# Products of the second transform step over both parts at once, and a filter spectrum split by channels between two homes

## The chip, the cores and the metric

The kernel runs on one core of a Trainium2 chip. In the profile the core shows as PE (TensorE: matmuls; PEld are its weight loads), DVE (VectorE), ACT (ScalarE), POOL (GpSimd) and SP, which here only issues DMA transfers. PSUM is used as eight banks of 512 fp32 values per partition. The metric is the device time of one execution in microseconds (us); a kernel's time is the median over its executions. All data are fp32.

## The reference

Two blocks follow each other. The first is a long convolution by FFT, with a filter that a small network makes from position embeddings; the second applies a wide layer with the activation h·cos(h) to each token.

```python
# x, v: (4, 12480, 128); pos_emb: (12480, 64); w1: (64, 64); w2: (64, 128)
h_filt = (np.maximum(pos_emb @ w1, 0.0) @ w2) * np.exp(-0.01 * pos)[:, None]
u = x * v
y = irfft(rfft(u, n=2*S, axis=1) * rfft(h_filt, n=2*S, axis=0)[None], n=2*S, axis=1)[:, :S]
a = (x * y).reshape(49920, 128)
h = a @ w_in                      # w_in: (128, 2048)
out = (h * np.cos(h)) @ w_out     # w_out: (2048, 128)
```

## The kernel before, in words

**The transform.** Sequence positions are taken as `R` = 104 rows of `N2` = 120. A transform has two matmul steps, of sizes `N1` = 96 and `N2` = 120, and two more lead back. The 128 channels are held as `CB` = 64 pairs (`b`), the two channels of a pair (`i`) beside each other. The filter keeps its first 10400 taps, in `FR` = 96 rows. Before the first step, sums and differences of mirrored positions are formed (`u_sums`, `filter_out`), so that the first step leaves `KE` = 124 rows: 0 to 63 from the sums, 64 to 123 from the differences.

**First step** (`f1_mm`, L400; evictions L415 and L424). For each pair two matmuls fill one bank with 96 frequencies `k`, real and imaginary part `r`, for both channels. ACT or DVE, chosen by `f1_takers`, copies it out: one copy for rows 0 to 63, and for rows 64 to 123 a copy and a negated copy, since the parts change places there. For data this goes to `parts`, columns 0 to 191 of the large tile `slots` (128 partitions x 64 pairs x 240 columns x 2). For the filter (`f1_evict_filter`) each pair's 192 columns are divided by frequency: 144 go to a separate tile `ftile`, and the last 48, the imaginary parts with `k` >= `KF` = 48, to `above`, the last 48 columns of `slots`. The filter's eviction therefore takes five instructions, two copies for the upper rows and three for the lower.

**Second step** (`f2_mm`, L437). For two frequencies `k1`, `k1+1` at a time (a unit `j`, 48 of them per batch), a weight tile `w` of 124 x 120 per frequency multiplies the 256 values of that frequency (2 parts x 64 pairs x 2 channels). The result of frequency `g` of the two stands in half `g` of a bank, ordered part, pair, channel. For the filter, one matmul does it where both parts lie in `ftile` (`k` < 48), and two of 128 columns where the imaginary part lies in `above`.

**The product** (`f2_product`, L451). With u the data's result in PSUM and h the filter's in SBUF, the complex product is written back over `parts`: four DVE multiplications of 256 values (two into the place of the result, y, two into a scratch tile `t`), and on POOL one subtraction and one addition of 256 values (L461). `t` has one buffer, and POOL's operation is issued right behind the second and the fourth multiplication.

**What runs in which order.** Every engine works through its own instructions in the order in which the program lists them. `units` (L514) interleaves the parts of a loop: in unit `j` it issues the preparation of unit `j + ahead`, the matmuls of `j`, and between them, at each `yield`, a piece of the eviction of `j - 1`. The program's stages are:

1. Loads of x and v for batch 0 and their product (`first_u`, on POOL and DVE), beside the filter's small network.
2. First step of the filter (L843 to L854): while `first_u` lasts, two pieces of it per piece of `first_u`; then the rest, with the tables of the way back (`inverse_tables`, computed by POOL, and by a Sin on ACT) put in between, and stored to DRAM (L269).
3. First step of batch 0 (L871), beside the conversion of `w_in` from double precision.
4. Second step of batch 0 and of the filter together (`f2_both_units`, L594). Per unit `make_w` makes the next unit's `w` in two buffers (two ACT and two DVE instructions, L289 and L291); `w` is stored to DRAM for the later batches (`wd`, L603), the filter's scaled spectrum is evicted by ACT (L614) and stored too (`hd`, L616), and the product follows. The tables of the way back were reloaded just before (`back_tables`, L874 to L876).
5. Way back of batch 0, first part (L889), beside the conversion of `w_out` and some tables for the second part.
6. The second block. Each of its steps has an up-matmul (L727), ACT L730, DVE L733, POOL L736, ACT L741, DVE L743 and a down-matmul (L752) four steps later. The convolution of the other batches is issued in between, by fixed step costs (`owed`, L942 to L944). There `f2_units` (L575) loads `w` and `h` again and makes the same product, 3 x 48 times.

Of the kernel before, what the change touches and what calls it, by code (L numbers as in the profile page):

```python
# [16 lines left out]
P = 128  # L17
# [13 lines left out]
def kernel(  # L31
# [62 lines left out]
    KF = N1 - 2 * (N2 - N1)  # L94
    CB = D // 2
    assert R * N2 == S and S + TAPS - 1 <= 2 * M and math.exp(DECAY * TAPS) < 2.0 ** -150
    assert D == P and DFF % P == 0 and FO * 2 == P and N1 % 2 == 0 and R <= P
    assert NCH * ROWS <= FR <= R and H <= ODD and KE <= N1 + KF and H <= CB and N2 <= P
# [5 lines left out]
    NALL = 1 + math.ceil((NROWS - R) / P)  # L104
    assert G == 2 * UA and H % UA == 0 and N2 % G == 0
# [4 lines left out]
    hd = dram.tile([N1 // 2, N2, 2, 2, D], F32, name="hd")  # L110
# [141 lines left out]
    def inverse_tables(pool):  # L252

        t = Tables(pool, nc.gpsimd, 4)
        part = t.whole([P, 1], [[1, 1]], channel_multiplier=1, name="part")
        part4 = t.whole([P, 1], [[1, 1]], base=1, channel_multiplier=4, name="part4")
        step = t.whole([P, P], [[1, P]], name="step")
        mid = t.whole([P, P], [[1, P]], base=-MID, name="mid")
        cs, rows, tw_t = back_tables(pool)
        yield from t.sines(step, part, N2, [(cs[:, 0, 0:H + 1], 1), (cs[:, 1, 0:H + 1], 0)],  # L260
                           eighths=slice(0, H + 1, H))
        yield from t.sines(step[:, 1:H], part, N2,
                           [(cs[:, 0, H + 1:], 0), (cs[:, 1, H + 1:], 1)])
        yield from t.sines(step, part4, 4 * N1,
                           [(rows[:, i, :], q) for i, q in enumerate((0, 1, 2, 3))])
        yield from t.sines(mid, part4, TURN, [(tw_t[:, 0, :], 1), (tw_t[:, 1, :], 0)],
                           eighths=slice(H - 1, N2, H))
        t.finish(len(t.waiting))
        for kept, made in ((csd, cs), (rowsd, rows), (twd, tw_t)):  # L269
            nc.sync.dma_start(kept[:, :, :], made[:, :, :])  # L270

    def back_tables(pool):

        cs = pool.tile([N2, 2, N2], F32, name="cs")
# [3 lines left out]
        return cs, rows, tw_t  # L278
# [97 lines left out]
    def clear_gap(u):  # L376

        nc.gpsimd.memset(u[:, :, H:ODD, :], 0.0)
# [45 lines left out]
    def f1_evict_filter(ps, b, share):  # L424

        copy, negated = f1_takers(b, share)
        pj = ps[:, 0:4 * N1].rearrange("p (i k) -> p k i", i=2)
        near, far = ftile[:, b, :, :], above[:, b, :, :]
        copy(out=near[0:ODD], in_=pj[0:ODD, 0:N1 + KF])
        copy(out=far[0:ODD], in_=pj[0:ODD, N1 + KF:])  # L430
        yield
        copy(out=near[ODD:KE, 0:N1], in_=pj[ODD:KE, N1:])
        negated(near[ODD:KE, N1:], pj[ODD:KE, 0:KF])
        negated(far[ODD:KE], pj[ODD:KE, KF:N1])
        yield

    def f2_mm(ps, w, k1, i, filt=False):  # L437

        k = k1 + i
        pi = ps[0:N2, i * 2 * D:(i + 1) * 2 * D]  # L440
        if not filt:
            nc.tensor.matmul(pi, w[:, i, :], parts[0:KE, :, k], start=True, stop=True)  # L442
        elif k < KF:
            both = ftile[0:KE, :, k:k + N1 + 1:N1, :].rearrange("p b r i -> p r b i")
            nc.tensor.matmul(pi, w[:, i, :], both, start=True, stop=True)
        else:
            for r, src in enumerate((ftile[0:KE, :, k, :], above[0:KE, :, k - KF, :])):
                nc.tensor.matmul(pi[:, r * D:(r + 1) * D], w[:, i, :], src,
                                 start=True, stop=True)

    def f2_product(pool, ps, h, k1):  # L451

        y = parts[0:N2, :, k1:k1 + 2, :, :].rearrange("p r k b i -> p r b k i")
        uu, hh = (a.rearrange("p g r (b i) -> p r b g i", i=2) for a in (
            ps[0:N2, :].rearrange("p (g r d) -> p g r d", g=2, r=2), h[:, :, :, :]))
        t = pool.tile([N2, 2, CB, 2, 2], F32, name="t", bufs=1)
        for r, op in ((0, ALU.subtract), (1, ALU.add)):
            nc.vector.tensor_tensor(y[:, r], uu[:, 0], hh[:, r], op=ALU.mult)
            yield
            nc.vector.tensor_tensor(t[:, r], uu[:, 1], hh[:, 1 - r], op=ALU.mult)  # L460
# [105 lines left out]
    def f1_units(bank, u, share=0.5, evict=f1_evict):  # L566
        def mm(j, ps, i):
            if i == 0:
                ps = bank()
            f1_mm(ps, u, j, i)  # L570
            return ps

        return units(CB, F1_STEPS, lambda j: None, mm, lambda j, ps: evict(ps, j, share), 2)

    def f2_units(bank):  # L575
        with tc.tile_pool(name="there", bufs=3) as pool:
            ws, hs = {}, {}

            def before(j):
                ws[j] = pool.tile([KE, 2, N2], F32, name="w")  # L580
                nc.sync.dma_start(ws[j][:, :, :], wd[j, :, :, :])
                hs[j] = pool.tile([N2, 2, 2, D], F32, name="h")
# [11 lines left out]
    def f2_both_units(bank):  # L594

        with tc.tile_pool(name="both", bufs=2) as pool:
# [15 lines left out]
            def after(j, ps):  # L612
                h = pool.tile([N2, 2, 2, D], F32, name="h", bufs=3)
                nc.scalar.activation(h[:, :, :, :].rearrange("p g r d -> p (g r d)"),  # L614
# [169 lines left out]
    with tc.manual_schedule():  # L784
        with tc.tile_pool(name="psum", bufs=8, space=PSUM) as psum, \
# [50 lines left out]
            ftile = fpool.tile([P, CB, N1 + KF, 2], F32, name="ftile")  # L836
            clear_gap(ftile[0:FR, :, :, :])
            with tc.tile_pool(name="out", bufs=1, side="right") as pool:
                for j in range(H // 2):
                    filter_out(pool, bank, aT, ftile, j, w2_sb)  # L840
                    for _ in range(1 + (j % 3 == 0)):
                        next(first_u)
            f1 = f1_units(bank, ftile[0:FR, :, :, :], 0.53, f1_evict_filter)  # L843
# [30 lines left out]
            cs, rows, tw_t = back_tables(lpool)  # L874
            for kept, here in ((csd, cs), (rowsd, rows), (twd, tw_t)):
                nc.sync.dma_start(here[:, :, :], kept[:, :, :])  # L876
# [4 lines left out]
            wpool = ctx.enter_context(tc.tile_pool(name="weights", bufs=1))  # L881
            ident = wpool.tile([P, P], F32, name="ident")
# [92 lines left out]
```

## Time and profile before

| | us |
|---|---|
| median of 7 executions | 3787.01 (3785.79 to 3789.98) |
| the profiled execution | 3786.39 |
| its span, first to last instruction | 3784.6 |
| first step of the filter | about 65 to 122 |
| first step of batch 0 | about 122 to 171 |
| second step of batch 0 and filter | about 172 to 275 |
| way back of batch 0, first part | about 275 to 340 |
| second block, with the other batches until about 2970 | 345 to the end |

The profile describes one execution. A row of a timeline reads: start, duration, engine, line, operation, what it writes and reads, its shape, and how many in a row; in brackets, how long the engine had been idle and what ended that. The chain of waits follows the work that ended last back from the end. A table by stretches of time gives each engine's busy time, the clock granted to PE, the mean busy share of the 16 DMA engines, and the data rate. PE's matmuls overlap and their ends are modelled, so that a short pause of PE can hide in its busy time; the distance from one start to the next is more exact.

### The profile page before, as it was taken

Reading aid. Unit: us, or ns where it says so; the run is one execution under the profiler, and the core shown is the slowest. Engines: PE = TensorE matmul, PEld = TensorE weight load, DVE = VectorE, ACT = ScalarE, POOL = GpSimd, SP = SyncE. Lnnn points to the kernel's source line nnn. Section 1 sums busy time; section 2 is a strip of 40 time slices with the busy share of each in tenths; the row PEclk is TensorE's granted clock in tenths of the full one; section 3 lists DMA queues with packets and bytes.
Section 4 is the critical chain, followed back from the end, with each engine's and each line's share of the span. In section 5 each row is a group of like instructions: output and inputs, shape, how many; then the busy total and the mean of one; then the engine's idle time right before and its main releaser. Section 6 shows DMA issues by size and latency. Waiting matters only on the chain.

```text
span 3784.6 us, 47244 instructions
## 1 busy us (share of the span) xinstructions
PE 3701.5 (98%) x13546; PEld 2109.7 (56%) x13546; DVE 2771.4 (73%) x5658; ACT 2523.7 (67%) x4683; POOL 2589.3 (68%) x2342
## 2 busy tenths in 40 slices
PE   7898999999999999999999999999999999999999
PEld 6777555655466555555565556555566544444444
DVE  7887887688866777788767786788765566666666
ACT  5757776766665557766655567666664677777777
POOL 7667886488854665688745664788644577777776
PEclk9999999999999999999999999999999999999999
DMA  6263542022202550122203540122105200000000
GB/s 166 67 181 105 148 147 58 17 71 79 74 18 67 175 163 28 32 78 77 60 18 109 173 128 16 53 76 78 41 12 167 88 19 21 17 20 20 17 21 14
DMA packets 209499, 276.14 MB, mean 73 GB/s; under 512 B 17111, under 2 KB 146535, under 8 KB 209111
## 3 DMA queue, kind: packets, MB, share of 16 engines
q1 hardware_dynamic: 209239, 273.12, 25.0%
q8 instruction: 109, 1.79, 0.2%
q14 instruction: 151, 1.24, 0.1%
HBM read 193.64 MB, written 79.42 MB: 72 GB/s over the span
## 4 chain that ended last, share of the span: by engine, by line
PE 83%; POOL 7%; DVE 3%; ACT 2%; DMA 2%; issue 2%; SPq 0%; POOLq 0%; DVEq 0%; ACTq 0%
PE ph L727 31%; PE acc L752 27%; PE cv L752 5%; PE cv L491 4%; PE cv L466 4%; POOL f L736 4%; PE cv L402 3%; PE cv L442 3%; PE ph L126 2%; PE ps L442 1%; PE ps L402 1%; POOL tm L295 1%; DMA tm<-td 1%; ACT cs L741 1%; DVE k L733 1%
## 5 line engine op out<-in xcount | busy, mean ns | idle before, releaser
L736 POOL TENSOR_TENSOR f<-a,k 128x512 f32<-128x512 f32 (+1 forms) x1568 | 1985.3, 1266 | 1054.5 <-DVE k L733 1049.9
L727 PE MATMUL ph<-at,w_in_sb 128*128 128x512 f32 (+1 forms) x3136 | 1599.0, 591 | 6.0 <-DVE gt L743 5.4
L730 ACT ACTIVATE a<-ph,quarter 128x512 f32<-128x512 f32 (+1 forms) x1568 | 1072.5, 684 | 759.3 <-PE ph L727 750.5
L752 PE MATMUL acc<-gt,w_out_sb 128*128 128x512 f32 (+1 forms) x2688 | 1375.1, 593 | 9.8 <-ACT ot L758 9.5
L743 DVE TENSOR_TENSOR gt<-ph,cs 128x512 f32<-128x512 f32 (+1 forms) x1568 | 1077.8, 687 | 317.8 <-ACT cs L741 290.3
L733 DVE TENSOR_SCALAR k<-a 128x512 f32<-128x512 f32 (+1 forms) x1568 | 770.1, 491 | 621.2 <-ACT a L730 605.3
L741 ACT ACTIVATE cs<-f 128x512 f32<-128x512 f32 (+1 forms) x1568 | 980.3, 625 | 331.7 <-POOL f L736 329.1
L752 PEld LDWEIGHTS acc<-gt,w_out_sb 128*128 128x128 f32 x2688 | 506.5, 189 | 661.7 <-issue 618.8
L727 PEld LDWEIGHTS ph<-at,w_in_sb 128*128 128x128 f32 x3136 | 554.2, 190 | 337.9 <-issue 268.4
L461 POOL TENSOR_TENSOR slots<-slots,t 120x256 f32<-120x256 f32 x384 | 311.3, 817 | 61.0 <-DVE t L460 38.3
L491 PEld LDWEIGHTS cv<-slots,tm 96*104 96x104 f32 x1920 | 239.5, 170 | 112.0 <-issue 82.1
L491 PE MATMUL cv<-slots,tm 96*104 96x128 f32 x1920 | 253.6, 274 | 12.4 <-DMA tm<-td 6.3
L752 PE MATMUL cv<-gt,w_out_sb 128*128 128x512 f32 (+1 forms) x448 | 224.6, 584 | 0.7 <-DVE gt L743 0.7
L466 PEld LDWEIGHTS cv<-cs,slots 120*96 120x96 f32 x1536 | 176.8, 167 | 67.5 <-issue 65.6
L466 PE MATMUL cv<-cs,slots 120*96 120x120 f32 x1536 | 183.1, 266 | 0.0
L442 PE MATMUL cv<-slots,w 124*120 124x256 f32 x576 | 173.1, 381 | 0.0
L442 PEld LDWEIGHTS cv<-slots,w 124*120 124x120 f32 x576 | 103.7, 184 | 123.7 <-issue 110.7
L402 PEld LDWEIGHTS cv<-c,slots 104*124 104x124 f32 x768 | 132.6, 192 | 71.1 <-issue 58.3
L402 PE MATMUL cv<-c,slots 104*124 104x192 f32 x768 | 151.3, 327 | 4.8 <-DVE gt L743 3.5
L752 PEld LDWEIGHTS cv<-gt,w_out_sb 128*128 128x128 f32 x448 | 84.9, 190 | 104.4 <-issue 99.5
L390 DVE TENSOR_TENSOR xt<-xt,vt 104x256 f32<-104x256 f32 x177 | 137.9, 786 | 0.2 <-DMA vt<-in_v_dram 0.2
L476 DVE TENSOR_TENSOR slots<-cv,other 96x240 f32<-96x240 f32 x384 | 133.5, 394 | 4.2 <-ACT other L474 4.2
(129 smaller groups left out, 2583.6 us busy)
## 6 DMA issues: line engine op xcount, KB each, us to landing
h<-hd SPq DMA_DIRECT2D x144, 240.0 KB
tm<-td SPq DMA_DIRECT2D x96, 312.0 KB
xt<-in_x_dram SPq DMA_DIRECT2D x120, 208.0 KB
vt<-in_v_dram SPq DMA_DIRECT2D x120, 208.0 KB
xs<-in_x_dram SPq DMA_DIRECT2D x120, 208.0 KB
zd<-zs SPq DMA_DIRECT2D x119, 208.0 KB
zb<-zd SPq DMA_DIRECT2D x96, 256.0 KB
w<-wd SPq DMA_DIRECT2D x144, 116.2 KB
```

Of the source, the lines that this page charges most:

```text
L402: nc.tensor.matmul(ps[0:KE, i * 2 * N1:(i + 1) * 2 * N1], u[:, b, 0:KE, i], c1[0:u.shape[0], :, :].rearrange("p r k -> p (r k)"), start=Tr ...
L442: nc.tensor.matmul(pi, w[:, i, :], parts[0:KE, :, k], start=True, stop=True)
L461: nc.gpsimd.tensor_tensor(y[:, r], y[:, r], t[:, r], op=op)
L466: nc.tensor.matmul(ps[0:N1, (i * 2 + r) * N2:(i * 2 + r + 1) * N2], parts[0:N2, r, :, b, i], cs[:, r, :], start=True, stop=True)
L491: nc.tensor.matmul(ps[0:R, i * D:(i + 1) * D], t[:, i, r, :], slots[0:N1, :, place, :], start=(r == 0), stop=(r == 1))
L727: nc.tensor.matmul(ph[:, 0:m], w_in_sb[:, c * P:(c + 1) * P], ats[n][:, 0:m], start=True, stop=True)
L730: nc.scalar.activation(a[:, 0:m], ph[:, 0:m], AF.Identity, bias=quarter[:, 0:1], scale=INV_TWO_PI)
L733: nc.vector.tensor_scalar(out=k[:, 0:m], in0=a[:, 0:m], scalar1=ROUND, scalar2=ROUND, op0=ALU.add, op1=ALU.subtract)
L736: nc.gpsimd.tensor_tensor(f[:, 0:m], a[:, 0:m], k[:, 0:m], op=ALU.subtract)
L741: nc.scalar.activation(cs[:, 0:m], f[:, 0:m], AF.Sin, scale=TWO_PI)
L743: nc.vector.tensor_tensor(gt[:, 0:m], ph[:, 0:m], cs[:, 0:m], op=ALU.mult)
L752: nc.tensor.matmul(accs[n][:, 0:m], w_out_sb[:, c, :], gt[:, 0:m], start=(c == 0), stop=(c == NFC - 1))
```

## The change

- **Product.** Two DVE multiplications of 512 values take the place of four of 256: one forms the result of u's real part with both parts of h, the other that of u's imaginary part with both parts in reversed order. Each reads its part of u from PSUM twice, through a pattern with a step of zero. POOL's two operations stay; both now come behind both multiplications, one `yield` apart. `t` gets two buffers.
- **Order in the bank.** The bank now holds part, pair, frequency, channel, so that what one multiplication reads is contiguous. Each second-step matmul therefore writes runs of two values at a distance of four. `h` in SBUF and `hd` in DRAM take the same order; their sizes stay.
- **Filter's first step.** The two homes are divided by channels: pairs 0 to 47 lie whole in `ftile` (`fout`), pairs 48 to 63 in `above`, each in four pieces. An eviction takes three instructions. The pairs are worked from 63 down, since `fout` lies over the memory of the inputs `fin`. A filter's second-step matmul is always two, of 192 and of 64 columns.
- **Tables.** Of the tables of the way back, only `cs` is reloaded before the joint second step; `rows` and `tw_t` are loaded after it, ahead of `w_in`.

```diff
     def f1_evict_filter(ps, b, share):
         copy, negated = f1_takers(b, share)
-        pj = ps[:, 0:4 * N1].rearrange("p (i k) -> p k i", i=2)
-        near, far = ftile[:, b, :, :], above[:, b, :, :]
-        copy(out=near[0:ODD], in_=pj[0:ODD, 0:N1 + KF])
-        copy(out=far[0:ODD], in_=pj[0:ODD, N1 + KF:])
+        pj = ps[:, 0:4 * N1].rearrange("p (i r q k) -> p r q k i", i=2, r=2, q=SPLIT // 2)
+        if b < NF:
+            there = fout[:, b, :, :].rearrange("p (r q k) i -> p r q k i", r=2, q=SPLIT // 2)
+        else:
+            there = above[:, (b - NF) * SPLIT:(b - NF + 1) * SPLIT, :, :].rearrange(
+                "p (r q) k i -> p r q k i", r=2)
...
+        copy(out=merged(there[0:ODD]), in_=merged(pj[0:ODD]))
         yield
-        copy(out=near[ODD:KE, 0:N1], in_=pj[ODD:KE, N1:])
-        negated(near[ODD:KE, N1:], pj[ODD:KE, 0:KF])
-        negated(far[ODD:KE], pj[ODD:KE, KF:N1])
+        copy(out=there[ODD:KE, 0], in_=pj[ODD:KE, 1])
+        negated(there[ODD:KE, 1], pj[ODD:KE, 0])
         yield
     def f2_mm(ps, w, k1, i, filt=False):
         k = k1 + i
-        pi = ps[0:N2, i * 2 * D:(i + 1) * 2 * D]
+        pi = ps[0:N2, :].rearrange("p (r b g i) -> p g r b i", r=2, g=2, i=2)[:, i]
         if not filt:
             nc.tensor.matmul(pi, w[:, i, :], parts[0:KE, :, k], start=True, stop=True)
-        elif k < KF:
-            both = ftile[0:KE, :, k:k + N1 + 1:N1, :].rearrange("p b r i -> p r b i")
-            nc.tensor.matmul(pi, w[:, i, :], both, start=True, stop=True)
-        else:
-            for r, src in enumerate((ftile[0:KE, :, k, :], above[0:KE, :, k - KF, :])):
-                nc.tensor.matmul(pi[:, r * D:(r + 1) * D], w[:, i, :], src,
-                                 start=True, stop=True)
+            return
+        nc.tensor.matmul(pi[:, :, 0:NF], w[:, i, :],
+                         fout[0:KE, :, k:k + N1 + 1:N1, :].rearrange("p b r i -> p r b i"),
+                         start=True, stop=True)
+        q, m = divmod(k, 2 * (N2 - N1))
+        far = above[0:KE, :, m, :].rearrange("p (b r q) i -> p q r b i", r=2, q=SPLIT // 2)
+        nc.tensor.matmul(pi[:, :, NF:], w[:, i, :], far[:, q], start=True, stop=True)
     def f2_product(pool, ps, h, k1):
-        y = parts[0:N2, :, k1:k1 + 2, :, :].rearrange("p r k b i -> p r b k i")
-        uu, hh = (a.rearrange("p g r (b i) -> p r b g i", i=2) for a in (
-            ps[0:N2, :].rearrange("p (g r d) -> p g r d", g=2, r=2), h[:, :, :, :]))
-        t = pool.tile([N2, 2, CB, 2, 2], F32, name="t", bufs=1)
+        y = parts[0:N2, :, k1:k1 + 2, :, :].rearrange("p r k b i -> p r b (k i)")
+        t = pool.tile([N2, 2, CB, 4], F32, name="t", bufs=2)
+        for r, (dst, hh) in enumerate(((y, h[:, :, :, :]), (t[:, :, :, :], h[:, ::-1, :, :]))):
+            u = ps[0:N2, r * 2 * D:(r + 1) * 2 * D].rearrange("p (b j) -> p b j", j=4)
+            twice = bass.AP(tensor=u.tensor, offset=u.offset, ap=[u.ap[0], [0, 2], *u.ap[1:]])
+            nc.vector.tensor_tensor(dst, twice, hh, op=ALU.mult)
+            yield
         for r, op in ((0, ALU.subtract), (1, ALU.add)):
-            nc.vector.tensor_tensor(y[:, r], uu[:, 0], hh[:, r], op=ALU.mult)
-            yield
-            nc.vector.tensor_tensor(t[:, r], uu[:, 1], hh[:, 1 - r], op=ALU.mult)
             nc.gpsimd.tensor_tensor(y[:, r], y[:, r], t[:, r], op=op)
             yield
...
-            f1 = f1_units(bank, ftile[0:FR, :, :, :], 0.53, f1_evict_filter)
+            f1 = f1_units(bank, fin[0:FR, :, :, :], 0.53, f1_evict_filter,
+                          range(CB - 1, -1, -1))
...
-            cs, rows, tw_t = back_tables(lpool)
-            for kept, here in ((csd, cs), (rowsd, rows), (twd, tw_t)):
-                nc.sync.dma_start(here[:, :, :], kept[:, :, :])
+            cs = third_table(lpool)
+            nc.sync.dma_start(cs[:, :, :], csd[:, :, :])
             for _ in f2_both_units(bank):
                 pass
             first.close()
             wpool = ctx.enter_context(tc.tile_pool(name="weights", bufs=1))
+            rows, tw_t = last_tables(wpool)
+            for kept, here in ((rowsd, rows), (twd, tw_t)):
+                nc.sync.dma_start(here[:, :, :], kept[:, :, :])
```

## The prediction

> **What bounds the kernel now.** First the page's busy times and its chain, then the busy times by stretches: the first two lines below are joint second steps (DVE and DMA busy, PE waiting), the last two second steps inside the second block.
>
> ```profile
> PE 3701.5 (98%) x13546; PEld 2109.7 (56%) x13546; DVE 2771.4 (73%) x5658; ACT 2523.7 (67%) x4683; POOL 2589.3 (68%) x2342
> ...
> PE 83%; POOL 7%; DVE 3%; ACT 2%; DMA 2%; issue 2%; SPq 0%; POOLq 0%; DVEq 0%; ACTq 0%
> ```
>
> ```profile
> 190.00:220.00 30.00, 29.17 (x118) 19.86 (x117) 28.30 (x89) 17.96 (x43) 20.91 (x30) 1.00 0.62 180
> 220.00:243.00 23.00, 22.93 (x136) 18.83 (x135) 22.17 (x69) 14.20 (x36) 16.06 (x23) 1.00 0.61 179
> ...
> 755.00:825.00 70.00, 70.00 (x199) 35.68 (x198) 55.71 (x110) 46.17 (x75) 58.87 (x55) 1.00 0.24 69
> 825.00:895.00 70.00, 70.00 (x198) 35.44 (x197) 56.32 (x115) 46.65 (x74) 62.09 (x58) 1.00 0.27 77
> ```
>
> In the second block PE is busy 70.00 of 70 us while DVE does these products; three of the four batches lie there. So only what lies before about 350 us can shorten much, and I read the timeline of one joint second step, which shows what ends the waits:
>
> ```profile
> 241.91 0.60 ACT L614 ACTIVATE h<-ps 120x512 f32<-120x512 f32 x1 [1.01 <-DMA hd<-h]
> ...
> 243.82 0.59 DVE L291 SCALAR_TENSOR_TENSOR w<-even,tw_w,ps 124x120 f32<-124x120 f32 x2 [0.80 <-DMA wd<-w]
> 244.33 0.42 DVE L458 TENSOR_TENSOR slots<-ps,h 120x256 f32<-120x256 f32 x1
> 244.66 0.41 DVE L460 TENSOR_TENSOR t<-ps,h 120x256 f32<-120x256 f32 x1
> 244.99 0.41 DVE L458 TENSOR_TENSOR slots<-ps,h 120x256 f32<-120x256 f32 x1
> 245.22 1.43 POOL L461 TENSOR_TENSOR slots<-slots,t 120x256 f32<-120x256 f32 x2 [1.30 <-DVE t L460]
> 245.32 0.41 DVE L460 TENSOR_TENSOR t<-ps,h 120x256 f32<-120x256 f32 x1
> 245.84 0.59 DVE L291 SCALAR_TENSOR_TENSOR w<-even,tw_w,ps 124x120 f32<-124x120 f32 x2
> ```
>
> A unit takes 2.02 us (243.82 to 245.84), and three loops have that length. (a) DVE: w, w, four products, and a wait instruction, without a gap. (b) t: POOL 1.43, then t 0.42 (one buffer), then 0.17 of hand-over. (c) The store of `w`: its tile has two buffers, so `w` of unit j+2 waits until the store of unit j has landed. In the trace's landing records four reports end each such store (fifteen that of an h), the last 3.28 us after its issue; from unit 17 on every `w` starts 0.12 us after the last report of the store two units before. Around: 0.12 + 0.61 (both halves of `w` and the issue) + 3.28 = 4.01 for two units. And the packets under way fall below four at no time from 182 to 200 us and stand at exactly four for 7 to 11% of it: some four DMA engines never rest. An engine that serves both stores has 124 / 4 = 31 packets of 960 B at 44 ns and 120 / 15 = 8 of 2 KB at 84 ns in a unit: 2.04 us.
>
> The chain shows the rest: how the first step of the filter ends.
>
> ```profile
> 120.21 0.44 POOL turned L217
> ...
> 120.68 0.30 ACT tw_t L226
> ...
> 122.20 36.02 PE ps L402 x200
> ```
>
> POOL's tables (97.9 to 120.6, without a gap) hold a Sin on ACT, and two evictions behind that Sin hold PE.
>
> **The change, part by part.** Sums are against the profiled execution: 3786.39 us, span 3784.6 and 1.8 around it; the median, 3787.01, is 0.6 above it.
>
> *Products beside the second block.* Removed: per unit four multiplications of 0.415 (row L458/L460); added: two of 512 values. The nearest row, 128x512 with one operand in PSUM (L743), is 0.687. DVE is relieved of 4 × 0.415 − 2 × 0.687 = 0.29 us, 144 times, 41 us. On the path: nothing; PE covers it. If that cover were gone, DVE would still have 14 of 70 us free. POOL's two operations (0.73 to 0.86) now come one behind the other: they can hold the block's L736 for 1.7 instead of 0.86 us. In these stretches a down-matmul starts at least 2.8 us after its DVE result is there, so no PE wait: 0.
>
> *Joint second step, length of a unit.* (a) by start-to-start distances: the products took 0.34 + 0.33 + 0.33 + 0.42 and the wait 0.10; two of 512 take 0.60 + 0.68 + 0.10: 1.88 in place of 2.02. (b) goes, with the second buffer. (c) stays: the same stores of the same sizes, on the same queue. Late next is thus the store, and a unit remains 2.01. Ends: 0, and 0.13 × 44 units = 5.7 gained. I take 0.4, for the first five units alone: there the reports come after 2.8 to 2.9 us and DVE sets the pace (its w starts at 178.09, 180.02, 182.04). [...]
>
> *Its matmuls.* For k < 48 a pass of 256 columns (0.217 from start to start, L445) becomes one of 192 (0.162, L402) and one of 64, bounded by half of the 128-column pass (0.054) and all of it (0.109, L448): 0 to 0.054 more per pass, four per unit, at most 0.22. PE then needs 8 × 0.217 = 1.74 to 1.96 of the 2.01: 0, covered by the store. In the other 24 units two passes of 128 become the same two: no more than that. [...]
>
> *Strided writes to PSUM.* No row of the trace has a matmul that writes with gaps. Lower end 0: a moving operand read in pairs with gaps (L442, 256 columns, 0.217) costs what a contiguous one does (L352, 0.215). Upper end: twice, as if each pair cost two; 576 passes in the second block × 0.217 = 125 us. I take 0, by L442.
>
> *End of the joint step.* After the last `w` (268.33) three rounds of loop (b) follow; POOL ends at 275.34, and the way back waits for it. Without (b): last h at 270.96 to 271.56, products to 272.87, POOL 1.42 and 0.14: 274.43. −0.9; ends: 0 if h still comes late behind a store, −1.5.
>
> *Filter's first step.* DVE per pair, start to start: 0.37 + 0.25 + 0.28 + 0.17 + 0.29 = 1.37 (88.04 to 89.41); afterwards as in the evictions of data, which have the same three shapes: 0.56 + 0.28 + 0.36 = 1.20. ACT: 1.17 to 1.05. Times 31 and 33: 5.3 and 4.0 us. From 74 to 98 us DVE is busy for 23.24 of 24 us, and `u_sums` of batch 0 queues behind these evictions, which delays the loads of x and v and so POOL; 12 DVE evictions lie there: 12 × 0.17 = 2.0. The remaining 19 are hidden by POOL's tables, whose 22.8 us stay and only begin earlier. Behind the last Sin two ACT evictions: 0.2. Sum −2.2; ends 0 (the loads of v, 3.2 us each, hold POOL too, at 67, 72 and 78 us) and −5.5.
>
> *Tables.* Two transfers leave SP's queue ahead of the joint step, where the first `w` waits for ACT; two join it behind the last `hd` and ahead of `w_in`'s, 0.35 us of issue each. First reader: ACT at 278.66; they land about 2.4 us after issue (as at 171 us), before 277. `w_in` and the raw `w_out` come 0.7 later, read first at 283.12: 0; at worst +0.7.
>
> Sum: −2.2 − 0.4 − 0.9 = −3.5: 3782.9 for the profiled execution, 3783.5 for the median.
>
> **Rivals.** *Faster: the store is not the floor.* With landing after 2.85 us loop (c) takes 1.79 a unit, DVE's 1.88 rules: 5.7 more, 3777.8. For: units 2 to 5. Against: the engines that never rest. *No gain in the first step:* v's loads and POOL hold it as before; 3785.7. For: three load waits in the chain; against: DVE's closed row after 80 us. *Slower: PE writes PSUM in pairs more slowly.* At a tenth more, 576 × 0.022 = 12.5: 3796. It decides from 19 ns a pass on (11 us, the 3.5 gained and 7.6 of bound). For: no row excludes it. Against: a pass takes 0.85 ns per column whatever the pattern it reads (L442, L352, L448). *The products shorten the second block:* 41 us of DVE, but PE has no idle time there to give: no price.
>
> **How the numbers follow.** Chances: forecast 0.52, no gain in the first step 0.17, store not the floor 0.19, slow writes 0.12. What a measurement can tell from no change is 0.2%, 7.6 us: below 3779.4 or above 3794.6. Faster: 0.19 and the forecast's edge where the first step gains all 5.5 and the end 1.5, 0.05: 0.24. Slower 0.12. Same 0.64. The forecast's own range is 3779 to 3787; for 8 in 10 it is opened to 3775, past most of the faster case, and to 3790, with 0.12 left out above and 0.06 below.
>
> **What would show it.** After: L458's successor at 120x512, 0.68 us, 384 of them; joint step still 2.0 us a unit, `w` waiting for `wd<-w` with longer idle time on DVE (some 0.13 a unit); no t wait for POOL; POOL's last operation there 1 us sooner after the last `w`; POOL's tables starting near 96 us; L442's passes 0.217 apart. Wrong if L442's distance grows, or if a unit falls below 1.95.

## The result, and the profile after

The kernel after the change takes 3799.16 us (median of 11 executions, 3795.78 to 3803.88), the kernel before 3788.1 us on the same chips. The ratio is 1.0030, with a 95% interval of 1.0022 to 1.0038: the change costs 0.3%, about 11 us, where 3.5 us of gain were forecast. The profiled execution of after is the slowest of the eleven, 3803.88 us with a span of 3802.1, so its timeline holds 4.7 us more than the median.

The page of after, first the busy times of the engines, then the shares of the chain that ended last:

```profile
PE 3714.0 (98%) x13642; PEld 2131.3 (56%) x13642; DVE 2759.5 (73%) x5212; ACT 2507.5 (66%) x4617; POOL 2587.8 (68%) x2342
...
PE 74%; POOL 12%; DVE 5%; ACT 3%; DMA 3%; issue 2%; SPq 0%; POOLq 0%; DVEq 0%; ACTq 0%
```

DVE's work shrank by 12 us, not by 41: the second block's products became cheaper as expected (238.4 to 195.7 us), but operations beside them took longer (k, DVE L746, 504 ns instead of 491 in the mean, 20 us over the run). More telling is the chain: PE's share fell from 83% to 74%, POOL's rose from 7% to 12%. On its last chain the kernel now stands behind POOL more often.

The same stretches as before the change, again with PE, PEld, DVE, ACT, POOL busy, the granted clock, DMA share and GB/s:

```profile
190.00:220.00 30.00, 29.94 (x181) 27.56 (x181) 26.59 (x60) 17.04 (x46) 21.21 (x30) 1.00 0.62 182
220.00:243.00 23.00, 22.33 (x133) 20.53 (x133) 19.71 (x45) 12.53 (x34) 15.62 (x22) 1.00 0.60 176
755.00:825.00 70.00, 69.10 (x195) 34.65 (x194) 54.58 (x89) 44.33 (x73) 57.89 (x53) 1.00 0.24 69
825.00:895.00 70.00, 69.23 (x196) 34.85 (x195) 54.71 (x89) 44.71 (x73) 60.03 (x57) 1.00 0.26 75
```

PE was busy 70.00 of 70 us in the second block; now 0.8 to 0.9 us are missing from each such stretch, and 4 and 2 matmuls from its count. The first two rows carry less DVE work (26.59 us for 28.30), and the step is no faster for it.

**Where the time went.** In the second block PE has the same list of instructions in both kernels, so the start of the n-th up-matmul after, minus its start before, is the lead or lag at that step. It reads −5.7 us where the way back begins (269.00 against 274.71), −3.7 at the way back's 256th pass, −2.2 at the first up-matmul, −1.3 at step 40 and at step 140, then +3.6 at step 320, +2.0 at 520, +6.6 at 660, +10.4 at 880, +15.3 at 1012, +17.5 at 1060, and +17.5 to the end. Early gains of 5.7 us were given back to 1.3; then 18.8 us were lost while the other batches ran.

Most of that loss falls on one place. A token tile takes 16 steps. Taking the start-to-start differences by position in the tile, steps 140 to 320, 520 to 660 and 880 to 1060 lose 4.85, 4.67 and 4.86 + 2.22 us = 16.6 us at positions 3 and 4, and nothing (0.0 us in each) at the other fourteen. The rest, 3.4 us between steps 760 and 880 and −1.6 between 320 and 520, differs from run to run: four other kernels with 512-wide products (spaced, store, raw_first and apart below) show +0.0, −0.9, +0.5 and +2.5 us in the first of these. Most of the 3.4 us lies at one place, steps 767 and 768, where PE waits 2.1 us for the load of a table (`cv <- DMA tm<-td`) instead of 0.9.

Positions 3 and 4 are the border of two tiles. There PE runs the last down-matmul of a tile, ACT copies the accumulator out (`ot`, L771), and the next tile's first down-matmul needs the same bank, since `acc` has only one. PE's waits in the second block while the other batches run, before and then after (total us, number, longest):

```profile
PE acc L752 <- ACT ot L758: 9.5, 16, 1.5
PE cv L491 <- DMA tm<-td: 6.3, 6, 2.1
PE ph L727 <- DVE gt L743: 5.4, 9, 1.5
```

```profile
PE acc L765 <- ACT ot L771: 18.5, 27, 2.2
PE ph L740 <- DVE gt L756: 7.2, 10, 1.5
PE cv L503 <- DMA tm<-td: 5.7, 7, 2.1
```

One border, step 196, first before the change, then after it (start, us, engine, line, operation; in brackets the idle time before and what ended it):

```profile
808.34 1.27 POOL L736 TENSOR_TENSOR f<-a,k 128x512 f32<-128x512 f32 x1 [0.36 <-DVE k L733]
...
809.64 0.63 ACT L741 ACTIVATE cs<-f 128x512 f32<-128x512 f32 x1
...
810.18 0.57 ACT L758 COPY ot<-acc 128x512 f32<-128x512 f32 x1
...
810.98 1.02 PE L752 MATMUL acc<-gt,w_out_sb 128*128 128x512 f32 x2
```

```profile
806.69 1.27 POOL L749 TENSOR_TENSOR f<-a,k 128x512 f32<-128x512 f32 x1 [0.87 <-DVE k L746]
...
807.92 0.93 POOL L473 TENSOR_TENSOR slots<-slots,t 120x256 f32<-120x256 f32 x1
...
808.81 1.28 POOL L749 TENSOR_TENSOR f<-a,k 128x512 f32<-128x512 f32 x1
...
810.12 0.63 ACT L754 ACTIVATE cs<-f 128x512 f32<-128x512 f32 x1 [0.92 <-POOL f L749]
810.66 0.57 ACT L771 COPY ot<-acc 128x512 f32<-128x512 f32 x1
...
811.28 1.13 PE L765 MATMUL acc<-gt,w_out_sb 128*128 128x512 f32 x2 [0.75 <-ACT ot L771]
```

Before, the copy comes in time at this border. After, `f` stands behind a product operation of 0.93 us, the cosine waits 0.92 us for `f`, `ot` stands behind the cosine in ACT's list, and PE stops for 0.75 us. The chain of after near this border reads

```profile
808.85 1.25 POOL f L749
810.10 0.02 issue
810.12 0.63 ACT cs L754
810.75 0.48 ACT ot L771
811.23 0.04 issue
811.28 1.13 PE acc L765 x2
```

and the chain of before is PE alone from 800 to 815 us. The tables below use the distance from the last down-matmul's start of one tile to the first one's of the next, which includes pauses hidden in PE's modelled busy time. Over the 29 borders in steps 140 to 320, 520 to 660 and 880 to 1020 it is 2.74 us before and 3.24 after: 29 × 0.505 = 14.6 us. Borders in the other stages of the convolution (3.20 and 3.21) and those after it (2.32 and 2.32) did not change. PE's first down-matmul of a tile starts 0.05 us behind the end of `ot` at 19 of these 29 borders before, and at 25 after: the copy was the last to be waited for in most places already.

### The profile page after: what moved, and what is told of

Its sections match the earlier page's. It is cut to its first block, busy times and chain, and to the rows that moved or that the text cites. A ratio compares the mean times of both kernels' runs of the same rounds, so it can differ in the third digit from the quotient of the medians.

```text
span 3802.1 us, 46879 instructions
## 1 busy us (share of the span) xinstructions
PE 3714.0 (98%) x13642; PEld 2131.3 (56%) x13642; DVE 2759.5 (73%) x5212; ACT 2507.5 (66%) x4617; POOL 2587.8 (68%) x2342
## 4 chain that ended last, share of the span: by engine, by line
PE 74%; POOL 12%; DVE 5%; ACT 3%; DMA 3%; issue 2%; SPq 0%; POOLq 0%; DVEq 0%; ACTq 0%
PE ph L740 28%; PE acc L765 24%; POOL f L749 7%; PE cv L765 5%; PE cv L503 4%; PE cv L478 4%; PE cv L407 3%; POOL slots L473 2%; PE cv L454 2%; PE ph L129 2%; ACT cs L754 2%; DMA wd<-w 1%; DVE k L746 1%; DVE gt L756 1%; DMA tm<-td 1%
## 5 line engine op out<-in xcount | busy, mean ns | idle before, releaser
L746 DVE TENSOR_SCALAR k<-a 128x512 f32<-128x512 f32 (+1 forms) x1568 | 790.4, 504 | 654.2 <-ACT a L743 632.8
```

What stands on the lines that cost most here:

```text
L746: nc.vector.tensor_scalar(out=k[:, 0:m], in0=a[:, 0:m], scalar1=ROUND, scalar2=ROUND, op0=ALU.add, op1=ALU.subtract)
```

## The experiments

Theory A of the expectations: POOL's two product operations, now one behind the other, delay `f`, so the cosine, so `ot`, so PE. Rival B: the late chain reaches PE through the ring of four up-matmul banks. Rival C: it is DVE's multiplications that delay the chain, not POOL. (A1 and C1 are the same two, put for one run.) Each time is the median of its run; the kernel before took 3786.8 us beside the first eight and 3787.6 beside the last four. It took 3788.1 beside after's 3799.2, so a difference to after carries up to 1.3 us of uncertainty from that alone.

### The copy ahead of the cosine: ot_first

```diff
-            if 0 <= i - 1 < len(steps):
-                gates[i - 1] = moe_act(mpool, *hidden.pop(i - 1))
-            if i >= LAG:
-                pn, pc = steps[i - LAG]
-                moe_down(pn, pc, gates.pop(i - LAG))
-                if pc == NFC - 1:
-                    ots[pn] = moe_evict(mpool, pn)
+            last = i >= LAG and steps[i - LAG][1] == NFC - 1
+            for down in ((True, False) if last else (False, True)):
+                if not down and 0 <= i - 1 < len(steps):
+                    gates[i - 1] = moe_act(mpool, *hidden.pop(i - 1))
+                if down and i >= LAG:
+                    pn, pc = steps[i - LAG]
+                    moe_down(pn, pc, gates.pop(i - LAG))
+                    if last:
+                        ots[pn] = moe_evict(mpool, pn)
```

> The kernel after the change, with one reordering: at the end of a token tile, the last down-matmul and ACT's copy of the accumulator (ot) are issued ahead of that step's cosine instead of behind it. Theory A: the change lost its time in the second block, about 19 us, because ACT's cosine waits for POOL's f, POOL is held by the two product operations that now follow each other, and ot stands behind that cosine while the next tile's first down-matmul needs the only accumulator bank. Then PE's waits 'acc <- ACT ot' (18.5 us in 27 waits after, 9.5 in 16 before) fall under 4 us and the time falls from 3799 to 3780 to 3787. Rival B: the late steps reach PE through the ring of four banks of the up-matmul ('ph <- DVE gt'), which ot has no part in: then 3796 to 3800, and the ot waits turn up as ph waits.

3782.73 us, ratio to before 0.9991 (0.9982 to 1.0000): 16.4 us faster than after by this order of two instructions per tile. The border distance falls from 3.24 to 2.77 us. PE's waits, and the same border:

```profile
PE ph L740 <- DVE gt L756: 11.1, 21, 1.5
PE cv L503 <- DMA tm<-td: 6.9, 7, 1.7
```

```profile
802.61 0.57 ACT L771 COPY ot<-acc 128x512 f32<-128x512 f32 x1
...
803.62 0.63 ACT L754 ACTIVATE cs<-f 128x512 f32<-128x512 f32 x1 [0.44 <-POOL f L749]
803.87 1.02 PE L765 MATMUL acc<-gt,w_out_sb 128*128 128x512 f32 x2
```

`ot` runs a microsecond ahead of the cosine and PE's `acc` wait is gone from the list. The steps themselves are as late as ever (up-matmul to the end of `gt` takes 6.12 us on average in these stretches, 5.89 after, 5.63 before). So the copy queued behind the cosine is a way in which lateness reaches PE. It is not the only one. The same reordering also gains 12.5 us in the kernel before (before_ot, below) and brings the border distance there to 2.52, where it stays at 2.77 here. In ot_first the waits `ph <- DVE gt` rose from 7.2 to 11.1 us, and 9.2 of these stand at the same border, at the up-matmul just ahead of the tile's first down-matmul: that is B's ring. How much goes which way is worked out from wide_all and narrow_all below.

### Which engine makes the chain late: spaced, close, apart, close2

Four pacings of the product, in the second block alone. First, POOL's operations as far apart as before the change:

```diff
             nc.vector.tensor_tensor(dst, twice, hh, op=ALU.mult)
-            yield
+            if r == 0 or not spaced:
+                yield
         for r, op in ((0, ALU.subtract), (1, ALU.add)):
             nc.gpsimd.tensor_tensor(y[:, r], y[:, r], t[:, r], op=op)
             yield
+            if r == 0 and spaced:
+                yield
```

> The kernel after the change; in the second block POOL's subtraction is issued right behind the second multiplication and its addition two pieces later, so that the two stand as far apart as before the change. The 512-wide multiplications stay. Theory A (POOL's two operations in succession): the second block's loss of about 19 us goes, 3780 to 3788, and PE's 'acc <- ACT ot' returns to about 9.5 us. Rival C (two DVE multiplications of 0.68 us stand in front of the block's k, where ones of 0.41 stood): 3796 to 3800.

3795.49 us, ratio 1.0024 (1.0014 to 1.0034): 3.7 us of the loss gone, not the whole. Theory A, as far as it names POOL alone, is wrong.

Then the opposite, the kernel before with four narrow multiplications in the pacing of after:

```diff
             nc.vector.tensor_tensor(y[:, r], uu[:, 0], hh[:, r], op=ALU.mult)
-            yield
             nc.vector.tensor_tensor(t[:, r], uu[:, 1], hh[:, 1 - r], op=ALU.mult)
-            nc.gpsimd.tensor_tensor(y[:, r], y[:, r], t[:, r], op=op)
             yield
+        for r, op in ((0, ALU.subtract), (1, ALU.add)):
+            nc.gpsimd.tensor_tensor(y[:, r], y[:, r], t[:, r], op=op)
+            yield
```

> The kernel before the change, with its four multiplications of 256 values; in the second block they are issued two by two, and POOL's two operations in the two pieces behind them, which is the pacing of the kernel after. Theory A: slower than before by what the second block lost, 15 to 20 us: 3803 to 3808 against 3788. Rival C (it is the 512-wide form that holds DVE): 3786 to 3791.

3836.25 us, ratio 1.0134. This one answers another question: `t` has one buffer in the kernel before, and in this pacing DVE has to wait for POOL to read it.

```profile
DVE t L461 <- POOL slots L467: 46.2, 41, 1.2
```

The same kernel with two buffers for `t` in the second block (`bufs=2 if close else 1`):

> As the kernel before the change with four multiplications issued two by two and POOL's operations in the two pieces behind, now with two buffers for t in the second block, so that the wait of the multiplication for POOL (46 us in the run with one buffer) is gone. DVE and POOL are then loaded piece by piece as after the change, with twice as many instructions half as wide. If what costs is how much work stands in one piece (A1 or C1), the border loss comes back: 3800 to 3808 against 3787. If it is the single instruction of 512 values that k cannot get past (width), 3786 to 3791.

3802.33 us, ratio 1.0041 (1.0028 to 1.0053); 15.5 us slower than before, with not one 512-wide instruction in the block. What costs is how the work is bunched; the width isn't needed for it. The remaining arrangement spreads DVE and leaves POOL's operations one piece apart:

```diff
             nc.vector.tensor_tensor(dst, twice, hh, op=ALU.mult)
-            yield
+            if r == 0 or not spaced:
+                yield
+            if r == 0 and spaced:
+                yield
```

> The kernel after the change; in the second block the two 512-wide multiplications are issued two pieces apart instead of one, POOL's two operations in the two pieces that follow (subtraction right behind the second multiplication). So DVE's load is spread as evenly as two instructions allow, POOL's two operations stay one piece apart. Theory A1 (POOL's two operations close together hold f): nothing gained, 3797 to 3801, the loss at the tile borders (16.6 us after; 11.9 with POOL's operations spread) stays. Theory C1 (two multiplications of 0.68 us close together hold k and gt): the border loss falls below 6 us, 3785 to 3791.

3806.76 us, ratio 1.0059 (1.0046 to 1.0072): slower than after, which neither had expected. The second multiplication and the subtraction that needs it now stand in one piece, so POOL waits at the head of its list, with `f` behind it. In spaced they stand so too; what apart has besides is the addition only one piece later. POOL's waits in the first of the stretches, 690 to 1045 us, after, then in spaced, then in apart:

```profile
POOL slots L473 <- DVE t L470: 5.4, 11, 0.5
```

```profile
POOL slots L474 <- DVE t L470: 11.4, 21, 0.7
```

```profile
POOL slots L476 <- DVE t L470: 12.8, 27, 0.5
```

All steps of the three stretches together, waits as 95th percentiles in us (worked out from the records of a, k and f of each step):

| kernel | k after a | f after k | a after its up-matmul's start | border distance (mean) | time |
|---|---|---|---|---|---|
| before | 0.48 | 0.57 | 1.25 | 2.74 | 3787 to 3788 |
| after | 0.99 | 1.24 | 1.86 | 3.24 | 3799.2 |
| spaced | 0.97 | 0.57 | 1.70 | 3.10 | 3795.5 |
| apart | 0.66 | 1.25 | 2.18 | 3.46 | 3806.8 |
| close2 | 1.12 | 1.25 | 1.81 | 3.18 | 3802.3 |
| narrow (below) | 0.49 | 0.57 | 1.27 | 2.74 | 3782.4 |

The change lengthened two tails: DVE's (k behind multiplications of 0.68 us, two in a row) and POOL's (f behind two operations in a row). `spaced` brings the second back to 0.57 and leaves the first, and keeps 12 of 16.6 us of border loss. `apart` shortens the first and leaves the second, but adds the wait of POOL for DVE. A late `f` also makes the `a` of a later step late, as it stands behind the cosine in ACT's list. So A and C are both true, and DVE's part is the larger: spaced and narrow (below) issue POOL's two operations in the same pieces, and spaced is 13.1 us slower. An exact division isn't settled, since spaced and apart both brought a wait of POOL for DVE (11.4 and 12.8 us against 5.4), and in spaced only the tail of `f`'s wait fell, not its mean (0.34 us, 0.33 after, 0.28 before).

### The product alone put back: narrow

```diff
+        if narrow:
+            for r, op in ((0, ALU.subtract), (1, ALU.add)):
+                for s, dst in enumerate((y, t)):
+                    u = ps[0:N2, s * 2 * D:(s + 1) * 2 * D].rearrange("p (b j) -> p b j", j=4)
+                    nc.vector.tensor_tensor(dst[:, r], u, h[:, r ^ s, :, :], op=ALU.mult)
+                    if s == 0:
+                        yield
+                nc.gpsimd.tensor_tensor(y[:, r], y[:, r], t[:, r], op=op)
+                yield
+            return
```

> The kernel after the change, with the second block's product put back to four multiplications of 256 values and POOL's operations behind the second and the fourth, as before the change; bank order, strided writes, joint step, filter's first step and tables stay as after. If the product beside the second block is the whole cause, the border loss of 16.6 us goes and the early gain (1.3 us ahead at the 40th step) stays: 3783 to 3787. If the strided writes or the order in the bank cost something there, more than 3790.

3782.42 us, ratio 0.9989 (0.9980 to 0.9998). The border loss is gone (2.74 us), PE's wait for `ot` is back at 9.6 us in 15 waits, and from step 140 to the end the lead over before stays between 3.1 and 4.3 us. The 512-wide product beside the second block costs 16.8 us (3799.2 − 3782.4; 15.5 if each is taken against the kernel before beside it), and everything else in the change together brings 4.4 us.

### The first step alone: split

The kernel before with the new `f1_evict_filter`, its order of pairs and the 192 + 64 matmuls; product, bank order and tables unchanged:

```diff
-        copy(out=near[0:ODD], in_=pj[0:ODD, 0:N1 + KF])
-        copy(out=far[0:ODD], in_=pj[0:ODD, N1 + KF:])
+        copy(out=merged(there[0:ODD]), in_=merged(pj[0:ODD]))
...
-        copy(out=near[ODD:KE, 0:N1], in_=pj[ODD:KE, N1:])
-        negated(near[ODD:KE, N1:], pj[ODD:KE, 0:KF])
-        negated(far[ODD:KE], pj[ODD:KE, KF:N1])
+        copy(out=there[ODD:KE, 0], in_=pj[ODD:KE, 1])
+        negated(there[ODD:KE, 1], pj[ODD:KE, 0])
```

> The kernel before the change with one part of the change alone: the filter's first-step results divided by channels (three eviction instructions in place of five, pairs from 63 down, second-step matmuls of 192 and 64 columns). Product, bank order and tables as before. After the whole change the joint second step began 5.6 us sooner. If that is this part's doing and it arrives at the end, 3782 to 3784; if the way back and the second block give some of it back, as after the change (5.7 us ahead at the way back, 1.2 at its 35th step), 3785 to 3788. The joint step's unit stays 2.02 us.

3784.49 us, ratio 0.9995 (0.9986 to 1.0004): by the times alone no different from before. In the trace batch 0's last first-step pass comes at 162.36 instead of 167.06 us, the first up-matmul at 342.30 instead of 345.79, and the lead at the last up-matmul is still 4.5 us.

### The store of w: store

```diff
-                nc.sync.dma_start(wd[j, :, :, :], ws[j][:, :, :])
+                for p in (slice(0, 112), slice(112, KE)):
+                    nc.sync.dma_start(wd[j, p, :, :], ws[j][p, :, :])
```

> The kernel after the change, with the store of w in two transfers, of rows 0 to 111 and of rows 112 to 123, where one of 124 rows is served by four DMA engines by the prediction's reading. If that store is the floor of the joint second step, its landing falls from about 3.3 us to below 2.6, DVE's 'w <- DMA wd<-w' wait ends (8.5 us after), and the unit shrinks from 2.01 to 1.9 us, 4 to 6 us over the step; 3793 to 3796. If PE's matmuls (busy 29.94 of 30 us there) are the floor instead, the landing is shorter and the unit stays 2.0: 3798 to 3800.

3795.70 us, ratio 1.0025 (1.0016 to 1.0035), 3.5 us faster than after; the joint step, first to last `w`, takes 92.97 us instead of 97.50. Two units after the change, then with the store divided:

```profile
239.33 0.59 DVE L296 SCALAR_TENSOR_TENSOR w<-even,tw_w,ps 124x120 f32<-124x120 f32 x2 [0.22 <-DMA wd<-w]
...
239.84 0.69 DVE L470 TENSOR_TENSOR slots<-ps,h 120x512 f32<-120x512 f32 x1
...
240.44 0.68 DVE L470 TENSOR_TENSOR t<-ps,h 120x512 f32<-120x512 f32 x1
...
241.36 0.59 DVE L296 SCALAR_TENSOR_TENSOR w<-even,tw_w,ps 124x120 f32<-124x120 f32 x2 [0.23 <-DMA wd<-w]
```

```profile
235.76 0.59 DVE L296 SCALAR_TENSOR_TENSOR w<-even,tw_w,ps 124x120 f32<-124x120 f32 x2
...
236.33 0.69 DVE L470 TENSOR_TENSOR slots<-ps,h 120x512 f32<-120x512 f32 x1
...
236.94 0.68 DVE L470 TENSOR_TENSOR t<-ps,h 120x512 f32<-120x512 f32 x1
...
237.71 0.59 DVE L296 SCALAR_TENSOR_TENSOR w<-even,tw_w,ps 124x120 f32<-124x120 f32 x2
```

After, each `w` waits 0.22 us for the store of two units before, and a unit takes 2.03 (2.01 in the median). With the store divided the wait is gone and a unit takes 1.95 us. In the landing records the 112 rows end with 16 reports and the 12 rows with 12, the last of the 16 after 1.9 us in the median, where the single store had four, the last after 3.3. The store was the floor.

The next floor, at 1.95, is not DVE. Behind a late store DVE catches up, and there two `w` start 1.70 us apart (187.74, 189.45, 191.14), while PE's units stay 1.94 to 1.96 us apart from 174 us on. The first of the stretches above, with the store divided (busy PE in front, PE's clock third from the right):

```profile
190.00:220.00 30.00, 30.00 (x187) 27.68 (x186) 28.48 (x63) 17.13 (x46) 22.45 (x32) 1.00 0.70 194
```

PE's passes of one frequency, from start to start, are 0.268 and 0.218 for the data and 0.163, 0.163, 0.056 and 0.105 for the filter: 0.97 us, twice a unit. In the kernel before four passes of 0.217 made 0.87. The extra 0.05 us of the first data pass comes behind the 64 columns in split as well, whose matmuls write without gaps, so it isn't the new order in the bank.

### The loads behind the joint step: raw_first

The load of `w_in` moves from ahead of the way back into `some_groups`, behind the first three raw pieces of `w_out`:

```diff
-            nc.sync.dma_start(w_in_sb[:, :], wind[:, :])
             beside(i1_units(bank), [(w_out_sb[:, c, :], w) for c, w in out_pieces], some_groups)
...
     def some_groups(pool):
+        nc.sync.dma_start(w_in_sb[:, :], wind[:, :])
```

> The kernel after the change; the load of w_in (1 MB) is issued behind the first three raw pieces of w_out instead of ahead of them. After the change DVE waits 1.4 us for the first raw piece at the start of the way back (none before), and the way back's lead falls from 5.7 to 4.2 us there. If the transfers ahead of raw are the reason, that wait ends and the lead at the 256th pass of the way back grows from 3.7 to about 5 us; in the time 1 to 2 us, 3797 to 3799. If rows and tw_t, which stay ahead, do it alone, the wait stays above 1 us.

DVE's first reading of a raw piece, after and then here:

```profile
279.66 0.29 DVE L136 TENSOR_SCALAR power<-raw 128x256 uint32<-128x256 uint32 x1 [1.40 <-DMA raw<-in_moe_w_out_dram]
```

```profile
279.81 0.28 DVE L136 TENSOR_SCALAR power<-raw 128x256 uint32<-128x256 uint32 x1
```

The wait is gone. The way back's lead shrinks by 1.0 us over its first 256 passes (4.4 to 3.3), by 2.0 after the change (5.7 to 3.7); the lead itself was smaller from the start in this run, so the expected 5 us is not reached. The time, 3798.02 us (ratio 1.0027), differs from after's by no more than the runs spread.

### What the two kernels can be brought to: before_ot, wide_all, narrow_all

before_ot is the kernel before with the reordering of ot_first alone.

> The kernel before the change, with only the copy of the accumulator (and the last down-matmul ahead of it) issued before that step's cosine. In the profile of before PE waits 9.5 us for that copy, in 16 waits. If the tile border is a place where PE waits in the kernel before too, most of this goes: 3778 to 3782 against 3787, and the distance from the last down-matmul of a tile to the first of the next (2.73 us on average in the stretches of the second step) falls to about 2.6. If the copy's delay only turns into another wait there: 3785 to 3788.

3775.04 us, ratio 0.9968 (0.9956 to 0.9981): 12.5 us faster than before, more than expected. The border distance falls to 2.52 us beside second steps, and from 3.20 to 3.07 in the other stages. The border cost PE time in the kernel before already, more than the 9.5 us its waits show. PE's `ph <- DVE gt` waits rise only from 5.4 to 6.9 us.

wide_all is after with the edits of ot_first, store and raw_first together.

> The kernel after the change (512-wide product everywhere) with three edits together: the accumulator's copy ahead of the cosine, the store of w in two transfers, w_in behind the first raw pieces. If the gains add up: 3799.2 - 16.5 (the copy) - 3.5 (the store) - 1.5 (raw) = 3777.7; 3775 to 3781.

3776.38 us, ratio 0.9972 (0.9960 to 0.9983). The gains add up within 1.3 us.

narrow_all is wide_all with the product of narrow.

> As the run with the three edits, and the second block's product as before the change (four multiplications of 256). 3782.4 (that product alone) - 3.5 - 1.5 and what the copy still costs there, about 5: 3772 to 3777. If the wide product costs nothing once the copy is out of the way, the two runs agree within 2 us; if the longer chain still reaches PE elsewhere, this one is 3 to 5 us the faster.

3767.91 us, ratio 0.9951 (0.9937 to 0.9965): faster than both kernels, 19.6 us under before. It is 8.5 us faster than wide_all, more than expected: beside second steps the border distance is 2.52 against 2.76, and PE's `ph <- DVE gt` waits are 6.8 us against 10.8. At the up-matmul of the border there are 16 such waits against 7. So with the copy out of the way the bunched product still costs 8.5 of its 16.8 us, about half, and most of it at the same border: 7.8 of the 9.7 us that the two profiles' second-step stretches differ by lie at positions 3 and 4. The other half goes by way of the copy.

## Why the prediction was wrong

**Products beside the second block: 0. This step failed**, at its path. It said that POOL's pair can hold L736 for 1.7 us, which the trace confirms in kind (95th percentile of f's wait from 0.57 to 1.24 us), and then looked for whom that holds: the down-matmul, whose slack behind its DVE result it put at 2.8 us at least. Nearly so: the least is 2.67 us in these stretches before and 2.09 after, so no down-matmul waits for `gt` there. But one in sixteen, the first of a tile, waits for a bank as well, and the bank for ACT's `ot`, which stands behind the very cosine that waits for `f`. Nothing in the prediction says who is queued behind that cosine. Nor does it look at who else waits for `gt`: an up-matmul needs the bank that `gt` is formed from, and is short of it at the same border. By wide_all and narrow_all about half of the loss goes each way. The profile of before had it: `PE acc L752 <- ACT ot L758`, 9.5 us, is the longest of PE's waits in that stage. "PE is busy 70.00 of 70 us" was read as cover, but a busy share doesn't say how much room is left at one border in sixteen steps. The step also named only POOL; DVE, which it took to be relieved, had two 0.68 us instructions in a row where four shorter ones had been spread, and delays `k`. The step was put at nothing and measured +16.8 us.

**The joint step's unit: right, its ends not.** A unit stays at 2.01 us, and the store is why (before the change the packets under way do fall to three, for 0.2% of 182 to 200 us, but no lower); divided, it gives 1.95, and the last `w` starts 4.4 us sooner (259.12 for 263.53). The prediction read from the landing reports that four engines carry the 124 rows, and divided the store goes with that reading: 16 reports for 112 rows where the whole had four, landed after 1.9 us in the median for 3.3, the wait gone. Why 124 rows come to four no run shows; that 112 would come to more was the author's estimate, and no other division was run. The rival that had DVE's loop rule next, at 1.88 us, is wrong too: that loop runs in 1.70 where it catches up, and PE's passes rule at 1.95. The prediction took 0.60, 0.68 and 0.10 for the products and a wait; two 512-wide ones follow each other 0.60 us apart, and the 0.10 is gone where DVE is late. A single multiplication of 512 values took 680 to 690 ns, as put. Two instructions fewer save little: operations of 256 values follow each other after 0.33 to 0.34 us and those of 512 after 0.60, so a merged pair saves 0.06 to 0.08 us, about 0.14 a unit as the prediction's distances gave. The 0.4 us of the first units did not come: the first eight took 17.2 us for 16.5 before. At the start PE's clock is at half (0.50 until 172.3 us, before until 176.6), and the 192 and 64 columns take 0.95 us from start to start there for 0.85. Just behind these units a store landed late once (0.85 us of wait at 185.94). From first to last `w` the step grew from 96.71 to 97.50 us.

**Its matmuls and strided writes: right, 0.** PE's passes of a unit went from 1.74 to 1.95 us, almost the 1.96 put as the upper end, and stayed under the store's 2.01. A data pass of 256 columns takes 0.220 us from start to start in the second block in both kernels (0.217 in the shortest tenth). The rival of slow writes falls; that it had the right sign and nearly the right time, 3796, is luck.

**End of the joint step: right.** From the last `w` to the first pass of the way back 6.38 us became 5.47: −0.9.

**The filter's first step: right in kind, too small.** POOL's tables end 2.0 us sooner, as put:

```profile
118.25 0.44 POOL turned L220
118.71 0.30 ACT tw_t L229
...
120.12 9.92 PE ps L407 x49
```

but the step called the other evictions hidden behind the tables. They were not: when the last Sin ends PE has started 272 passes instead of 260, and 12 × 0.18 us (the mean of the 200 passes behind it before) is 2.2 more; and ACT's two evictions behind it are shorter, 1.05 us each for 1.17. Batch 0's first step ended 5.6 us sooner after, 4.7 in split: at the far end of the range, 5.5, where −2.2 was taken.

**Tables: +0 to 0.7 was too low.** The two loads, with `w_in` behind them, delay the raw pieces, 1.4 us of DVE wait; raw_first shows that `w_in`'s place ends it.

Without the failed step the sum comes out near, −4.4 us in narrow, which has every other part, against −3.5. That is partly luck: the first step brought 4.7 to 5.6 us for 2.2, and the joint step (0.8 us longer instead of 0.4 shorter), the tables and PE's clock at the way back's second part took most of the surplus again.

## What to carry to other kernels

Where an engine is called covered, follow the late result past its reader to whatever stands behind that reader in its engine's list, and look there for the rare instruction that returns a single buffer: here once in 16 steps, and by it and the up-matmul beside it the change lost its time. Fewer and longer instructions were no gain here to engines that a tight loop shares, since they bunched the work: `narrow` kept the four short ones and was 16.8 us faster. And when a wait of PE is already on the list, such as 9.5 us for one copy, try the order of the two instructions first: that alone made the old kernel 12.5 us faster.

## What was not expected of the hardware

The time at which PE's clock was granted in full again didn't follow from its pause alone. Before and after the change PE idles 4.87 us ahead of the first passes of the way back's second part. Stretches behind it, before (clock in the third column from the right), then after:

```profile
340.00:342.00 2.00, 1.91 (x9) 1.91 (x10) 0.62 (x3) 1.47 (x6) 1.33 (x2) 0.50 0.79 222
...
344.00:346.00 2.00, 1.41 (x13) 1.17 (x12) 0.56 (x1) 0.51 (x2) 0.63 (x1) 1.00 0.65 195
```

```profile
337.00:339.00 2.00, 2.00 (x10) 2.00 (x11) 0.62 (x2) 1.47 (x5) 1.27 (x2) 0.50 0.66 197
...
347.00:349.00 2.00, 2.00 (x5) 0.92 (x4) 0.00 (x0) 0.51 (x1) 0.62 (x1) 0.50 0.00 0
```

The clock is back at 343.9 us in one and is still at 0.50 up to 349.8 in the other, 4 and 13 us after the pause, though in the second PE is busy 2.00 of 2 us from 337 to 343 by the profile. In narrow, behind the same 4.88 us, it stays at half until 348.1, 13 us as well. Why is open. The lead shrank by 2.3 us over the first two up-matmuls; 1.7 came back at step 20, when before's clock fell to half once more, from 388.2 to 391.6 us.
